# A scan followed by a mixture of adapters: one store more goes out in pieces, in a new order of work

## The chip, the cores and the metric

The kernel runs on one core of a Trainium2 chip. The metric is the device time of one execution in microseconds (us). The time before is the median of three runs, 202.56 us (202.31 to 202.83). An engine here is TensorE (PE, with its weight loads PEld), VectorE (DVE), ScalarE (ACT), GpSimd (POOL) or SyncE (SP). Sixteen DMA engines move the data; SP issues the transfers.

## The reference

```python
def _attn_ref(a, b):                      # a, b: (8, 6400, 128) float32
    h = np.zeros((B, D), dtype=np.float32)
    for t in range(S):
        h = a[:, t] * h + b[:, t]
        out[:, t] = h
    return out

def _moe_ref(x, w_gate, A, B):            # x: (51200, 128), 8 experts of rank 16
    logits = x @ w_gate
    topk = np.argpartition(-logits, K, axis=1)[:, :K]        # K = 2
    sel = np.take_along_axis(logits, topk, axis=1)
    w = np.exp(sel - sel.max(-1, keepdims=True))
    w /= w.sum(-1, keepdims=True) + 1e-09
    for e in range(E):
        for k in range(K):
            mask = topk[:, k] == e
            delta[mask] += w[mask, k, None] * (x[mask] @ A[e] @ B[e])
    return x + delta
```

A linear recurrence along 6400 steps for eight sequences gives 51200 rows of 128 values. Each row then goes through the two adapters that its gate picks, and their sum is added to it. The inputs a and b are 26.2 MB each, the output is 26.2 MB.

## The kernel before

The 51200 rows are cut into 100 chunks of 512 rows. A chunk goes through these steps. Names in parentheses are those of the kernel's operations, with the chunk's number behind them.

- SP loads a and b (la, lb, line 709), mostly for two chunks at a time, 512 KB each, into rings of six buffers.
- PE transposes them by products with a unit matrix (A, B, P, line 730), so that the 128 features lie on partitions and time along the free axis.
- ACT copies the transposed a out of PSUM (ae, line 748), and DVE runs the recurrence with its scan instruction (sc, line 786) from a_st and PSUM into xT. A scan needs the last column of the one before.
- PE multiplies xT by the eight A matrices and the gate (Z, line 806), ACT copies the products out (ze, line 812) in units of four or six blocks of 128 rows.
- A group of up to four units is gated: the two largest logits of a row are found and turned into weights in some eight small steps (g on DVE, q on POOL, w1 on ACT, lines 843 to 882).
- POOL or DVE multiplies the products by the weights (mu or md, lines 915 and 919), PE transposes that (T, line 928), ACT or DVE copies it to zwT (te, lines 934 and 937), PE adds xT and the adapters' outputs in PSUM (D, lines 942 and 943), ACT or DVE copies the sum into the ring outt (oe or od, lines 957 and 954).
- SP stores two chunks at a time, 512 KB, the last four chunks one by one (st, line 988). The store of chunks 80 and 81 is called store 80 below.

The order of the work on each of the five queues is worked out when the kernel is built. Every operation has a rank: the start of its period of six chunks, plus a number from `TEMPLATE` by its kind and its place in the period, plus a number of its own from `NUDGE`. `Program.schedule` walks through the operations with an estimated duration for each and, on each queue, takes the operation of the lowest rank among those still to be issued, with a window of zero. So the ranks alone decide the order on a queue, and the operations wait for each other by semaphores. Lists such as `TE_ACT`, `OE_DVE` and `GATE_DVE` say which engine does a copy or a step of the gating.

A store reads 128 partitions of outt; from each, two pieces of 2 KB, one for each chunk. `SPLIT` cuts a store by partitions into several DMAs, issued one after another by SP and counted on one semaphore. Before the change it holds store 68 alone, cut into 124 and 4 partitions:

```python
cuts = SPLIT.get(c, [128])
lows = [sum(cuts[:i]) for i in range(len(cuts))]

def send():
    all = [eng["sp"].dma_start(dst[p : p + n], view[p : p + n]) for p, n in zip(lows, cuts)]
    return all if len(all) > 1 else all[0]
```

At the end of SP's queue stand the waits for all stores. SP's last entries before the change are: lb98, then the stores 64, 68 (two DMAs), 66, 70, 72, 74, 76, 78, 80, 82, 84, 86, 90, 88, 92, 94, 98, 97, 99 and 96.

Of the kernel before, what the change touches and what calls it, by code (L numbers as in the profile page):

```python
# [218 lines left out]
EARLY = -400  # L219
LEAD = [1, 2]  # L220
TAPER = [2, 1, 1, 1, 1]
GATE_DVE = ['2_0', '2_14', '2_18', '3_1', '3_11', '3_13', '3_15', '3_16', '3_2', '3_8', '5_14', '5_17', '6_0', '6_18', '6_3', '7_1', '7_17', '7_18', '7_20', '7_21']
TAIL_UNITS = [4, 4, 4, 4]
HEAD_UNITS = [4, 4, 4]
FLAT = []
# [3 lines left out]
OE_DVE = [11, 15, 72, 81, 92, 94, 97]  # L229
# [13 lines left out]
SPLIT = {68: [124, 4]}  # L243
# [863 lines left out]
```

## Time and profile before

| what | value |
|---|---|
| median of three runs | 202.56 us (202.31 to 202.83) |
| the profiled execution: its time | 202.71 us |
| the profiled execution: its span, first to last instruction | 200.9 us |
| granted TensorE clock | 0.992 |
| busy PE / PEld / DVE / ACT / POOL | 179.4 / 156.7 / 175.8 / 175.7 / 136.6 us |
| DMA: moved, mean rate over the span | 79.26 MB, 395 GB/s |
| read from HBM, written to it | 52.56 MB, 26.21 MB |

The span is what the rows of the profile add up to. The time of the run also holds what lies before the first and behind the last instruction, 1.8 us here. A row of an engine gives line, engine, operation, the tile written and the tiles read, their shapes, the count, the busy time, the mean duration and the idle time of the engine before it with what ended it. A row of SP's queue marks the issue of a DMA, not its transfer; an issue's duration includes the time for which SP was held up in it. "To landing" is from the start of an issue until the last of the sixteen DMA engines has reported.

### The profile page before, as it was taken

The numbers are of one execution on the slowest core, as the hardware profiler recorded it, in microseconds if no ns is written. First come the engines' busy times: TensorE is split into PE (matmuls) and PEld (weight loads), VectorE is DVE, ScalarE is ACT, GpSimd is POOL, SyncE is SP. The second block draws the span as 40 slices with busy tenths as digits, with TensorE's granted clock in tenths as the row PEclk, the third lists the DMA queues.
The fourth block names the chain that finished last, engine by engine and source line by source line (L and its number), as shares of the span: only waits on it lengthen the run. The fifth ranks groups of instructions, "written<-read, shape, count | busy, mean of one in ns | idle before, by whom it ended". The sixth has DMA issues, their size and how long they took to land.

```text
span 200.9 us, 7616 instructions
## 1 busy us (share of the span) xinstructions
PE 179.4 (89%) x3192; PEld 156.7 (78%) x3192; DVE 175.8 (88%) x283; ACT 175.7 (87%) x327; POOL 136.6 (68%) x176
## 2 busy tenths in 40 slices
PE   6988888999899989996998999889999998998970
PEld 6876767888678878886887888778887887887850
DVE  1599899999999988998797999898899999999970
ACT  2479898999879989998897999899989998999870
POOL 1331549598999988697787797867956657867320
PEclk9999999999999999999999999999999999999996
DMA  6999999999999999999999999999999999999985
GB/s 211 399 410 405 407 409 402 409 409 404 420 400 402 393 415 404 408 413 411 408 412 409 410 409 416 413 409 410 412 410 409 417 411 408 402 385 385 373 339 203
DMA packets 29065, 79.26 MB, mean 395 GB/s; under 512 B 2664, under 2 KB 2920, under 8 KB 29032
## 3 DMA queue, kind: packets, MB, share of 16 engines
q1 hardware_dynamic: 28456, 78.39, 98.9%
q8 instruction: 25, 0.41, 0.8%
q10 hardware_dynamic: 576, 0.40, 0.6%
q14 instruction: 8, 0.07, 0.1%
HBM read 52.56 MB, written 26.21 MB: 392 GB/s over the span
## 4 chain that ended last, share of the span: by engine, by line
DMA 33%; PE 28%; ACT 8%; DVE 8%; issue 1%; SPq 1%; ACTq 0%
DMA a_tm<-in_a_dram 26%; DMA b_tm<-in_b_dram 7%; PE pO L942 5%; PE pZ L806 4%; PE pB L730 4%; PE pA L730 4%; DVE xT L786 4%; PE pO L928 4%; PE pO L943 4%; ACT zl L812 3%; ACT a_st L748 2%; ACT outt L957 2%; ACT zwT L934 1%; DVE zwT L937 1%; SPq L709 1%
## 5 line engine op out<-in xcount | busy, mean ns | idle before, releaser
L786 DVE TENSOR_TENSOR_SCAN xT<-a_st,xT,pB 128x512 f16<-128x512 f32 x96 | 120.5, 1255 | 6.5 <-PE pA L730 2.9
L915 POOL TENSOR_TENSOR zw<-zl,g 128x512 f16<-128x512 f32 x88 | 92.7, 1066 | 26.5 <-DVE g L882 19.3
L730 PE MATMUL pB<-ident_f,b_tm 64*128 64x64 f32 (+1 forms) x784 | 69.6, 230 | 6.1 <-DMA a_tm<-in_a_dram 5.6
L730 PE MATMUL pA<-ident_f,a_tm 64*128 64x64 f32 (+1 forms) x784 | 69.7, 230 | 0.6 <-DMA b_tm<-in_b_dram 0.3
L748 ACT COPY a_st<-pA 128x512 f32<-128x512 f32 x100 | 62.9, 634 | 4.9 <-PE pA L730 3.6
L730 PEld LDWEIGHTS pB<-ident_f,b_tm 64*128 64x128 f32 (+1 forms) x784 | 56.7, 139 | 11.1 <-DMA a_tm<-in_a_dram 7.3
L812 ACT COPY zl<-pZ 128x816 f32<-128x816 f32 (+1 forms) x69 | 59.6, 863 | 2.4 <-PE pZ L806 2.3
L730 PEld LDWEIGHTS pA<-ident_f,a_tm 64*128 64x128 f32 (+1 forms) x784 | 56.8, 139 | 6.1 <-DMA b_tm<-in_b_dram 0.7
L957 ACT COPY outt<-pO 128x512 f32<-128x512 f32 x87 | 55.0, 641 | 2.5 <-PE pO L943 2.2
L942 PE MATMUL pO<-ident_h,xT 128*128 128x128 f16 x368 | 51.4, 222 | 1.3 <-ACT zwT L934 1.1
L943 PE MATMUL pO<-cst_h,zwT 128*128 128x128 f16 x368 | 50.3, 219 | 0.0
L942 PEld LDWEIGHTS pO<-ident_h,xT 128*128 128x128 f16 x368 | 40.3, 113 | 4.4 <-ACT zwT L934 1.6
L806 PE MATMUL pZ<-cst_h,xT 128*128 128x136 f16 x400 | 36.0, 225 | 4.0 <-DVE xT L786 2.0
L943 PEld LDWEIGHTS pO<-cst_h,zwT 128*128 128x128 f16 x368 | 36.8, 100 | 0.0
L928 PE MATMUL pO<-ident_h,zw 128*128 128x128 f16 x368 | 35.2, 220 | 1.4 <-DVE outt L954 0.5
L806 PEld LDWEIGHTS pZ<-cst_h,xT 128*128 128x128 f16 x400 | 26.2, 115 | 8.6 <-DVE xT L786 4.2
L928 PEld LDWEIGHTS pO<-ident_h,zw 128*128 128x128 f16 x368 | 22.7, 97 | 4.9 <-issue 1.3
L937 DVE COPY zwT<-pO 128x512 f16<-128x512 f16 x57 | 23.0, 409 | 4.0 <-PE pO L928 3.6
L934 ACT COPY zwT<-pO 128x512 f16<-128x512 f16 x35 | 21.8, 627 | 4.4 <-PE pO L928 4.0
L852 POOL TENSOR_TENSOR L<-k,m 128x192 f32<-128x192 f32 (+2 forms) x16 | 8.3, 519 | 6.5 <-DVE m L850 6.5
L874 POOL TENSOR_TENSOR k<-k,L 128x192 f32<-128x192 f32 (+1 forms) x17 | 9.4, 554 | 4.5 <-DVE L L870 3.2
L848 POOL TENSOR_TENSOR L<-L,k 128x192 f32<-128x192 f32 (+1 forms) x15 | 8.6, 576 | 5.4 <-DVE L L845 4.7
(58 smaller groups left out, 113.3 us busy)
## 6 DMA issues: line engine op xcount, KB each, us to landing
a_tm<-in_a_dram SPq DMA_DIRECT2D x48, 512.0 KB, 13.1
b_tm<-in_b_dram SPq DMA_DIRECT2D x48, 512.0 KB, 13.2
out_dram<-outt SPq DMA_DIRECT2D x47, 512.0 KB, 13.1
a_tm<-in_a_dram SPq DMA_DIRECT2D x4, 256.0 KB, 4.2
out_dram<-outt SPq DMA_DIRECT2D x4, 256.0 KB, 4.0
b_tm<-in_b_dram SPq DMA_DIRECT2D x3, 256.0 KB, 5.7
out_dram<-outt SPq DMA_DIRECT2D x1, 496.0 KB
b_tm<-in_b_dram ACTq DMA_DIRECT2D x1, 256.0 KB, 3.4
```

The lines of the kernel that those rows point to most:

```text
L730: last = eng["pe"].transpose(*args)
L748: lambda: eng["act"].copy(a_st[c % NA][:, :], pA[:, c % 2, :]), fr(c, "ae"))
L786: last = eng["dve"].tensor_tensor_scan(out=x[:, s0:s1], data0=a_st[c % NA][:, s0:s1], data1=pB[:, c % 2, s0:s1], initial=init, op0=ALU.mul ...
L806: last = eng["pe"].matmul(pZ[:, k // (n // 2), o : o + W], xblock(b0 + k), Awg_h)
L812: return eng["act"].copy(zl[:, zb : zb + n, :].rearrange("p (h k) w -> p h (k w)", h=2), pZ[:, :, 0 : n // 2 * W])
L915: lambda: eng["pool"].tensor_tensor(out=wv, in0=zv, in1=gv, op=ALU.mult), ba(gi, c, "mu"))
L928: last = eng["pe"].transpose(ptile[:, k * 128 : k * 128 + 128], zz[:, k, :], ident_h[:, :])
L934: lambda: eng["act"].copy(zt, ptile[:, 0 : n * 128]), ba(gi, c, "ta"))
L937: lambda: eng["dve"].tensor_copy(zt, ptile[:, 0 : n * 128]), ba(gi, c, "te"))
L942: eng["pe"].matmul(dst, xblock(b0 + k), ident_h[:, :], start=True, stop=False)
L943: last = eng["pe"].matmul(dst, zt[:, k * 128 : k * 128 + 128], B_h, start=False, stop=True)
L957: lambda: eng["act"].copy(ov, bv), ba(gi, c, "oe"))
```

## The change

Store 80 goes out as five DMAs, of 112, 4, 4, 4 and 4 partitions, one behind the other on SP. The numbers in `TEMPLATE` and `NUDGE` are others for nearly every operation of the chunks 0 to 14 and 81 to 99; in between most `NUDGE` numbers are kept. Three lists change by a few entries:

```diff
-GATE_DVE = ['2_0', '2_14', '2_18', '3_1', '3_11', '3_13', '3_15', '3_16', '3_2', '3_8', '5_14', '5_17', '6_0', '6_18', '6_3', '7_1', '7_17', '7_18', '7_20', '7_21']
+GATE_DVE = ['2_0', '2_14', '2_17', '2_18', '3_1', '3_11', '3_13', '3_15', '3_16', '3_8', '5_14', '6_1', '6_18', '6_3', '7_17', '7_18', '7_20', '7_21']
-TE_ACT = [0, 1, 2, 6, 7, 11, 12, 19, 22, 24, 25, 30, 31, 36, 37, 42, 43, 48, 49, 54, 55, 59, 60, 61, 67, 68, 69, 73, 75, 78, 80, 82, 83, 87, 92, 93, 95, 96, 97, 98]
+TE_ACT = [0, 1, 2, 3, 6, 7, 11, 12, 19, 22, 24, 25, 30, 31, 36, 37, 42, 43, 48, 49, 54, 55, 59, 60, 61, 67, 68, 69, 73, 75, 78, 80, 82, 83, 87, 90, 92, 94, 95, 96, 97, 98]
-OE_DVE = [11, 15, 72, 81, 92, 94, 97]
+OE_DVE = [11, 15, 72, 81, 92, 93, 97]
-SPLIT = {68: [124, 4]}
+SPLIT = {68: [124, 4], 80: [112, 4, 4, 4, 4]}
 TEMPLATE = {
-    "la": [0.617, 1.382, -0.181],
-    "lb": [0.289, -1.881, 0.376],
+    "la": [1.746, 3.64, 1.589],
+    "lb": [1.687, 4.099, 0.505],
...
```

In the order that results, SP's queue is the same from the loads of chunk 66 on but for single places: the stores 66 and 70 stand ahead of 68, and store 94 ahead of 92. Its beginning is another: the loads of chunks 1 to 4 change places, store 0 goes out one pair of loads earlier, the stores 6 to 32 are spread otherwise among the loads of the chunks 34 to 64. On PE, DVE, ACT and POOL the order in the middle changes by single places; from chunk 88 on, the copy zwT of chunk 90 moves from DVE to ACT, the copies te and oe of chunks 93 and 94 exchange engines, of gating group 17 step 2 moves from POOL to DVE and step 5 from DVE to POOL.

More of the change, by code (lines that the diff above doesn't have):

```diff
@@ L242 @@
 STORE_TAIL = [1, 1, 1, 1]
-SPLIT = {68: [124, 4]}
+SPLIT = {68: [124, 4], 80: [112, 4, 4, 4, 4]}
 TOP8 = 4
 TEMPLATE = {
-    "la": [0.617, 1.382, -0.181],
-    "lb": [0.289, -1.881, 0.376],
-    "A": [0.0, 0.0, 0.0, 0.0, -22.609, 0.0],
-    "B": [0.016, -0.127, 0.808, 0.22, 0.59, 0.13],
-    "ae": [0.478, 0.108, 0.156, -0.214, 0.098, 0.802],
-    "sc": [-0.352, 0.601, 0.068, 1.247, 29.666, -1.078],
-    "Z": [0.074, 0.124, 0.07, -0.415],
-    "ze": [0.146, 0.091, -0.438, 0.663],
-    "g1": [0.736],
-    "g2": [-2.194],
-    "g3": [-0.858],
-    "g4": [-0.178],
-    "g5": [18.025],
-    "g6": [22.851],
-    "w1": [-0.215],
+    "la": [1.746, 3.64, 1.589],
+    "lb": [1.687, 4.099, 0.505],
+    "A": [0.0, 0.0, 0.0, 0.0, -31.987, 0.0],
+    "B": [0.376, -0.259, 0.365, 0.223, 0.306, 0.283],
+    "ae": [0.288, 0.221, -0.565, -0.575, -0.748, 1.3],
+    "sc": [-1.218, -1.749, -0.677, 0.613, 73.34, -1.523],
+    "Z": [0.196, 0.307, -0.011, -0.479],
+    "ze": [0.568, -0.504, -0.295, 1.091],
+    "g1": [7.23],
+    "g2": [-13.685],
+    "g3": [-2.163],
+    "g4": [-1.781],
+    "g5": [37.108],
+    "g6": [2.612],
+    "w1": [-1.333],
     "w2": [0.0],
@@ L264 @@
     "p3": [0.0],
-    "mu": [1.432, -0.247, 0.712, 0.979, 0.638, 1.684],
-    "T": [-0.04, 0.011, 0.309, 0.056, 0.263, 0.069],
-    "te": [-0.194, -0.349, -1.1, 4.512, 0.878, -1.627],
-    "D": [0.293, 0.3, -0.403, 0.26, 0.471, 0.206],
-    "oe": [-0.17, -1.066, 0.732, 0.378, -0.33, -0.315],
-    "st": [2.655, 0.241, 1.338],
-    "ta": [0.113, -0.235, -1.676, 1.106, 0.524, -0.261],
-    "md": [60.131, 24.961, 1.624, -2.633, 1.124, -17.851],
+    "mu": [2.792, 1.422, 1.022, 0.819, -2.419, 23.251],
+    "T": [-0.04, 0.099, 0.385, 0.077, -0.176, 0.11],
+    "te": [-1.747, -1.628, -1.308, 25.611, -20.775, -2.473],
+    "D": [0.087, -0.303, -0.762, 0.351, 0.059, 0.409],
+    "oe": [-0.455, -0.794, 0.928, 0.458, -0.076, -0.107],
+    "st": [13.665, 13.152, 11.84],
+    "ta": [2.542, -0.856, 2.005, 1.573, 0.74, 0.176],
+    "md": [104.08, 22.016, 10.978, -13.03, 11.367, -27.633],
     "wu": [0.0],
     "fi": [0.0, 0.0, 0.0, 0.0, 0.0, 0.0],
-    "ch": [53.69],
-    "cm": [11.639],
-    "cc": [8.728],
+    "ch": [122.022],
+    "cm": [101.955],
+    "cc": [20.929],
     "mb": [0.0],
-    "q2": [-0.491],
-    "q3": [-4.197],
-    "q5": [-3.568],
-    "q6": [0.447],
-    "q7": [0.367],
+    "q2": [0.509],
+    "q3": [-4.622],
+    "q5": [-4.987],
+    "q6": [-0.544],
+    "q7": [-7.111],
     "q8": [0.0],
-    "g7": [19.938],
-    "g8": [-0.285],
+    "g7": [33.274],
+    "g8": [-0.524],
 }
```

344 rows, old and new, of the table NUDGE are left out of this document.

## The prediction

> **What bounds the kernel now.** I read the page first, its strip of forty slices and its list of queues, then the windows of the tail, then SP's issues there, then the chain of waits.
>
> ```profile
> DMA  6999999999999999999999999999999999999985
> GB/s 211 399 410 405 407 409 402 409 409 404 420 400 402 393 415 404 408 413 411 408 412 409 410 409 416 413 409 410 412 410 409 417 411 408 402 385 385 373 339 203
> ...
> q1 hardware_dynamic: 28456, 78.39, 98.9%
> q8 instruction: 25, 0.41, 0.8%
> ...
> q14 instruction: 8, 0.07, 0.1%
> ```
>
> Five engines are busy for 68 to 89%, but the DMA engines are full from the second slice on: 78.39 MB move at about 410 GB/s, which is 191 us of a span of 200.9. Only the last five slices fall off. The row q8 matters below: 25 packets of instructions take 0.8% of sixteen engines' time, 0.008 x 16 x 200.9 / 25 = 1.03 us each, and each sits on one DMA engine.
>
> ```profile
> 160.00:170.00 10.00, 9.25 (x169) 7.84 (x167) 9.59 (x15) 9.03 (x18) 6.20 (x9) 1.00 1.04 413
> 170.00:175.00 5.00, 4.67 (x93) 4.09 (x91) 5.00 (x9) 5.00 (x10) 4.18 (x6) 1.00 1.01 401
> 175.00:180.00 5.00, 5.00 (x93) 4.52 (x90) 4.93 (x9) 4.96 (x11) 3.45 (x6) 1.00 1.03 385
> 180.00:185.00 5.00, 4.36 (x66) 3.68 (x65) 5.00 (x21) 4.92 (x11) 3.89 (x5) 1.00 1.04 395
> 185.00:190.00 5.00, 4.89 (x80) 4.29 (x78) 4.46 (x20) 4.43 (x11) 2.53 (x9) 1.00 0.95 365
> 190.00:195.00 5.00, 3.91 (x62) 3.27 (x60) 4.47 (x10) 3.46 (x8) 1.17 (x2) 1.00 0.89 340
> 195.00:198.00 3.00, 0.60 (x11) 0.42 (x8) 0.06 (x1) 1.07 (x2) 0.00 (x0) 0.95 0.81 313
> 198.00:201.00 3.00, 0.00 (x0) 0.00 (x0) 0.00 (x0) 0.00 (x0) 0.00 (x0) 0.50 0.36 139
> ```
>
> The columns are window, length, busy time of PE, PEld, DVE, ACT and POOL, clock, the mean share of the sixteen DMA engines, GB/s. From 185 us the mean share falls under one although stores are still outstanding: some DMA engines are out of work while others are not. That is an imbalance between the sixteen, and the changed split acts on nothing else.
>
> To see it, the sixteen semaphore updates of a DMA (one for each engine that has finished) are set out in order. This is counted from the trace's semaphore updates, in us; the first column is the issue's start:
>
> ```
> 164.60 store of 64       171.89 171.96 172.16 172.55 172.77 173.41 173.61 175.00 175.32 176.75 176.90 176.91 176.94 177.03 177.32 178.34
> 165.76 store of 68, 124  176.87 177.68 178.78 179.47   (four only)
> 166.23 store of 68, 4    177.08 177.88 178.96 179.66   (four only)
> 169.92 store of 66       173.13 173.39 173.79 176.24 176.69 178.00 178.16 178.17 178.18 178.31 178.31 178.57 179.11 179.75 180.19 180.92
> 170.55 store of 70       174.36 ... 180.39 181.12 181.47 182.20
> 192.20 store of 94       195.76 ... 196.59 196.89 197.62 197.85
> 197.10 store of 96       199.61 199.62 199.62 199.63 199.64 199.65 199.65 199.66 199.67 199.69 199.70 199.72 199.74 199.76 200.18 200.43
> ```
>
> Three things stand there. Before the split the sixteen engines are 6.4 us apart. Both pieces of store 68 run on four engines only, the same four (0.18 to 0.21 us between the two pieces on each), and those four were ahead before and are 178.3 to 180.92 after, so that the laggard at 180.92 is now one of them. At the end fourteen engines finish within 0.15 us (199.61 to 199.76), just behind the last issue, and two are late: 200.18 and 200.43. Followed from row to row, a store costs most engines 1.24 to 1.28 us, and one engine outside the four, which I call X, 1.38 to 1.41 (178.34, 179.75, 181.12). X overtakes by store 94 and is the 200.43; the slowest of the four is the 200.18. The span ends 0.47 us later, the run at 202.71, 1.81 above the span; the median of the three runs is 202.56, 0.15 below the profiled one.
>
> **The change part by part.** *The split of store 80.* It goes out as one piece of 112 partitions and four of 4.
>
> ```profile
> out_dram<-outt SPq DMA_DIRECT2D x47, 512.0 KB, 13.1
> ...
> out_dram<-outt SPq DMA_DIRECT2D x1, 496.0 KB
> ...
> out_dram<-outt SPq DMA_DIRECT2D x1, 16.0 KB
> ```
>
> A whole store gives each engine 8 partitions of 4 KB in 1.28 us, 0.16 us each. The trace has no piece of 112. Its bounds are the two rows: spread over sixteen as 128 is (7 partitions an engine), or over four as 124 is (28 an engine). I take sixteen, since 112 divides by 16 as 128 does and 124 does not. Every engine then saves 0.16 us (X 1.40 / 8 = 0.18). The four pieces of 4 all fall on the four: by data 4 x 0.16 = 0.64 us, by the measured 0.18 to 0.21 of the existing piece 0.72 to 0.84. I take 0.19 each, 0.76, the measured middle. The four get 0.76 - 0.16 = +0.60 us (0.48 to 0.68), the other twelve -0.16, X -0.18.
>
> In the Trainium skill, "DMA: Bandwidth & Descriptors", section "Why a DMA increments its semaphore by 16 and not by 1", a DMA takes the largest number up to 16 that divides the slowest dimension of both sides, on the lowest-numbered engines. The fours of updates above agree with it for 124 and 4; no row here shows it for 112, where it gives sixteen. [...]
>
> *SP's issues.* Four more of them.
>
> ```profile
> L988 SPq DMA_DIRECT2D out_dram<-outt x1: 3641/3641/3641, 166.2 to 166.2; - x1
> ...
> L988 SPq DMA_DIRECT2D out_dram<-outt x2: 1248/1329/1410, 178.9 to 180.2; - x2
> ...
> DMA to landing us min/median/max: 9.8/9.8/9.8
> ...
> L988 SPq DMA_DIRECT2D out_dram<-outt x2: 982/1050/1118, 195.9 to 197.1; - x2
> ...
> DMA to landing us min/median/max: 3.3/3.6/3.8
> ```
>
> The existing piece of 4 took 3.64 us to issue, behind 31 partitions for each of four queues; behind 7 partitions the first of the new ones should cost no more than an ordinary issue, and each of the others 0.35 to 0.5: some 2 us for SP at 180. Store 82, queued behind, takes 9.8 us from issue to landing against 3.3 for the last one, so some 6 us of queued work cover it on the slow engines. The fourteen quick ones do run dry, but end with the last issue at 197.10 anyway. If the cover were gone it would cost those 2 us. I count zero.
>
> *The new order on the five queues.* From the loads of chunk 66 on SP's order stands as before but for single places; ahead of that loads and stores change places by a few (store 0 goes out a pair of loads earlier, store 16 much earlier).
>
> ```profile
> 93.66 12.68 DMA a_tm<-in_a_dram
> ...
> 133.18 13.83 DMA a_tm<-in_a_dram
> ...
> 152.79 13.74 DMA b_tm<-in_b_dram
> ...
> 166.52 0.04 issue
> 166.57 0.27 PE pA L730
> ```
>
> The chain of waits comes back to a load again and again, for the last time at 166.57: compute has caught up with the loads there, and a load sits 12 to 14 us in the queue. A wait early in SP's queue has that queue as its cover; lost cover costs the length of the wait less that queue. So the early reordering counts zero, with no gain to be had either, as the DMA engines have no gap there.
>
> After 166.57 the chain is compute to the end, and there the moves are few: the copy of zwT of chunk 90 goes from DVE to ACT, 93 and 94 change engines for both copies, one step of a gating moves to POOL and another to DVE.
>
> ```profile
> L937 DVE COPY zwT<-pO 128x512 f16<-128x512 f16 x57 | 23.0, 409 | 4.0 <-PE pO L928 3.6
> L934 ACT COPY zwT<-pO 128x512 f16<-128x512 f16 x35 | 21.8, 627 | 4.4 <-PE pO L928 4.0
> ...
> 185.57 0.42 DVE L937 COPY zwT<-pO 128x512 f16<-128x512 f16 x1 [0.40 <-PE pO L928]
> 185.91 0.41 DVE L937 COPY zwT<-pA 128x512 f16<-128x512 f16 x1
> 186.46 0.42 DVE L937 COPY zwT<-pO 128x512 f16<-128x512 f16 x1
> ...
> 186.24 0.59 ACT L957 COPY outt<-pA 128x512 f32<-128x512 f32 x1 [0.36 <-PE pA L943]
> ```
>
> DVE loses 0.41 us, but stood waiting 0.40 us for PE just before; ACT gains 0.63, and has 0.36 of idle time there. The last issue moves by -0.4 to +0.3 us; I take zero. This counts only for the fourteen quick engines, which end at 199.76, 0.67 before the last.
>
> **The sum.** X: 200.43 - 0.18 = 200.25. The slowest of the four: 200.18 + 0.60 = 200.78 (200.66 to 200.86). The quick ones: 199.76 (199.4 to 200.1). The last landing goes from 200.43 to 200.78, +0.35, the profiled run to 203.06, the median to 202.9 (by the bounds 202.8 to 203.0).
>
> **The rivals.** A difference of 0.3%, 0.6 us, is about what a measurement of this kernel can tell from no change.
>
> *X stays last.* If the four come to store 80 with less lag, the end is X's 200.25: 202.56 - 0.18 = 202.4. For it: 173.41 and 173.61 in the row of store 64 become 178.78 and 179.47, 5.4 and 5.9 us for what cost the other two 4.9, so the laggard carries up to 1 us that need not come back. Against: the same kernel repeats within 0.5 us.
>
> *Faster.* The 25 packets of instructions hold one DMA engine each for 1.03 us, and queue q14's smaller ones less; which engine they hit makes the spread of 6.4 us. With a new order of instructions one can leave X, and another the slowest of the four: 200.25 - 1.03 = 199.2 and 200.78 - 0.95 = 199.8. The quick engines would decide together with the latter, 199.8: -0.63 us; with up to 0.4 from an earlier last issue, 201.8 in the middle. For it: fourteen engines are ready by 199.76. Against: it needs both at once.
>
> *Slower.* The same packet falls on the slowest of the four behind the split, while the late engines have no idle time left: 200.78 + 1.03 = 201.8, +1.4 us, 203.9. It decides from 0.6 us of extra wait on those four engines. For it: three such packets start after 176 us here (176.2, 181.9 and 191.0 by the trace's packet records), and the change makes four engines late instead of two. Against: two of the four have 0.4 us and more in hand.
>
> *It doesn't do what it says.* If the piece of 112 runs on four engines as 124 does, each gets 28 + 4 partitions instead of 8, 24 x 0.16 = 3.8 us: 204.0 against 200.43, +3.6 us, 206.1.
>
> **How the numbers follow.** Forecast 0.36, X stays last 0.08: together 0.44 for no difference over 0.3%. Faster 0.20. Slower 0.30 by a late packet and 0.06 by four engines, together 0.36. The likeliest is 202.9, its own range 202.4 to 203.2. With the rivals at 201.8 and 203.9 and the 0.1 to 0.2 us that single runs differ, 201.7 to 204.1; outside are the 0.06 at 206.1 and the ends of the rivals.
>
> **What would show it.** The page lists one more row of 448 KB and five rows or counts of 16 KB. The updates of the 112 piece come sixteen at a time (right) or four (the last rival). In the store of 96, two or more engines land late by 0.5 to 1.2 us behind the other twelve, and they are of the four that land the pieces of 4; if a single one is late, X has stayed last. The last issue of SP stands within 0.4 us of 197.1. Wrong would be a last issue later than 197.8, a gap in the DMA strip before slice 35, or all sixteen engines landing together.

## The result, and the profile after

The changed kernel takes 204.89 us (204.58 to 205.54, four runs) against 202.69 for the kernel before (202.31 to 202.83, four runs): a ratio of 1.0113, 95% interval 1.0091 to 1.0136. It is 2.2 us slower, and above the upper end of the forecast's range. Its profiled run took 205.54 us, with a span of 203.5 and a granted clock of 0.985.

The strips of the page's forty slices, after:

```profile
DMA  5999999999999999999999999999999999995995
GB/s 214 345 417 404 411 407 404 409 407 407 411 413 408 411 414 407 407 405 415 406 411 402 412 413 410 417 409 409 411 414 409 409 421 405 378 384 196 345 385 218
```

Where the kernel before ran down smoothly (385 385 373 339 203), there is now a hole of one slice, 196 GB/s, and after it the rate comes back to 385. The windows of the tail place it:

```profile
175.00:180.00 5.00, 5.00 (x93) 4.51 (x91) 4.97 (x9) 4.96 (x11) 4.14 (x6) 1.00 1.00 380
180.00:185.00 5.00, 4.40 (x66) 3.70 (x64) 5.00 (x21) 4.92 (x12) 3.62 (x5) 1.00 0.99 363
185.00:190.00 5.00, 4.57 (x80) 4.28 (x78) 4.13 (x19) 4.78 (x12) 2.53 (x9) 1.00 0.52 179
190.00:195.00 5.00, 3.94 (x62) 3.29 (x60) 4.47 (x11) 3.54 (x9) 1.26 (x3) 1.00 1.01 375
195.00:198.00 3.00, 0.68 (x13) 0.50 (x10) 0.13 (x1) 1.07 (x2) 0.00 (x0) 0.90 1.03 388
198.00:204.00 6.00, 0.00 (x0) 0.00 (x0) 0.00 (x0) 0.00 (x0) 0.00 (x0) 0.50 0.56 214
```

From 185 to 190 us the sixteen DMA engines are busy for 0.52 of the time, where they were for 0.95: 5 x 0.43 = 2.15 us lost. That is near the 2.2 us of the median, but the two need not be equal, since the rate behind the hole is higher than it was before (375 and 388 GB/s for 340 and 313). In the hole itself the last column says 179 GB/s for 365. The busy times of PE, DVE and ACT there differ from those before by 0.3 to 0.4 us, but the computation does not end late. The last copy into outt shows it, first before and then after:

```profile
195.67 0.59 ACT L957 COPY outt<-pA 128x512 f32<-128x512 f32 x1
...
195.75 0.59 ACT L957 COPY outt<-pA 128x512 f32<-128x512 f32 x1
```

It ends at 196.34, 0.08 later than before. What was late is SP's queue. Its rows at line 988 after, first the five DMAs of store 80, then everything from store 82 on (minimum, median and maximum of an issue in ns, start of the first and the last):

```profile
L988 SPq DMA_DIRECT2D out_dram<-outt x5: 947/1442/1840, 180.0 to 186.1; - x5
...
L988 SPq DMA_DIRECT2D out_dram<-outt x11: 468/1193/2118, 187.1 to 199.3; - x11
```

The five took 1.44, 1.84, 1.63, 1.01 and 0.95 us and held SP from 180.00 to 187.04. Before, store 80 was one issue of 1.25 us, and store 82 went out at 180.15. Now it goes out at 187.09, 6.94 us later. Behind it SP does not catch up: eleven issues follow one another with a median of 1.19 us and never wait for a copy, so that the last goes out at 199.33 instead of 197.10. The sixteen updates of the last store, in us:

```
before 199.61 ... 199.76 (fourteen) 200.18 200.43
after  201.76 ... 201.89 (eleven)   202.02 202.35 202.45 202.57 203.07
```

The quick engines end 2.2 us later, as the last issue does (2.23). The chain of waits does not show this: it ends in ACT's queue, at 195.72 after and 195.64 before, and follows no store.

The list of DMA issues after shows the split as written:

```profile
out_dram<-outt SPq DMA_DIRECT2D x14, 512.0 KB, 9.3
...
out_dram<-outt SPq DMA_DIRECT2D x1, 448.0 KB
out_dram<-outt SPq DMA_DIRECT2D x5, 16.0 KB
```

### The profile page after: what moved, and what is told of

It reads as the page before. It is cut to its first block, busy times and chain, and to the rows that moved or that the text cites. A ratio compares the mean times of both kernels' runs of the same rounds, so it can differ in the third digit from the quotient of the medians.

```text
span 203.5 us, 7626 instructions
## 1 busy us (share of the span) xinstructions
PE 179.8 (88%) x3192; PEld 156.3 (77%) x3192; DVE 174.5 (86%) x279; ACT 176.8 (87%) x329; POOL 138.4 (68%) x178
## 4 chain that ended last, share of the span: by engine, by line
DMA 26%; ACT 26%; PE 22%; DVE 11%; issue 4%; SPq 4%; POOL 3%; ACTq 0%; DVEq 0%
DMA a_tm<-in_a_dram 20%; ACT outt L957 8%; DVE xT L786 7%; ACT a_st L748 7%; ACT zl L812 6%; DMA b_tm<-in_b_dram 6%; ACT zwT L934 4%; PE pA L730 4%; PE pO L942 4%; PE pZ L806 4%; SPq L709 3%; PE pO L928 3%; PE pB L730 3%; PE pO L943 3%; POOL zw L915 3%
## 5 line engine op out<-in xcount | busy, mean ns | idle before, releaser
L957 ACT COPY outt<-pO 128x512 f32<-128x512 f32 x88 | 56.5, 650 | 2.9 <-PE pO L943 2.8
L937 DVE COPY zwT<-pO 128x512 f16<-128x512 f16 x55 | 22.3, 409 | 3.4 <-PE pO L928 3.2
L934 ACT COPY zwT<-pO 128x512 f16<-128x512 f16 x37 | 22.9, 627 | 2.0 <-PE pO L928 1.6
L874 POOL TENSOR_TENSOR k<-k,L 128x192 f32<-128x192 f32 (+2 forms) x18 | 9.7, 539 | 4.7 <-DVE L L852 3.6
L848 POOL TENSOR_TENSOR L<-L,k 128x192 f32<-128x192 f32 (+2 forms) x16 | 9.0, 564 | 4.3 <-DVE L L845 3.5
L786 DVE TENSOR_TENSOR_SCAN xT<-a_st,pB 128x512 f16<-128x512 f32 (+1 forms) x8 | 7.5, 937 | 4.6 <-PE pB L730 4.6
```

The lines of the kernel that those rows point to most:

```text
L786: last = eng["dve"].tensor_tensor_scan(out=x[:, s0:s1], data0=a_st[c % NA][:, s0:s1], data1=pB[:, c % 2, s0:s1], initial=init, op0=ALU.mul ...
L934: lambda: eng["act"].copy(zt, ptile[:, 0 : n * 128]), ba(gi, c, "ta"))
L937: lambda: eng["dve"].tensor_copy(zt, ptile[:, 0 : n * 128]), ba(gi, c, "te"))
L957: lambda: eng["act"].copy(ov, bv), ba(gi, c, "oe"))
```

## The experiments

Two kernels stand for "before's ranks" and "after's ranks"; the only line that is edited is `SPLIT`, and the ranks are all other lines of the diff. Every ratio is to the kernel before on the same chip, with its 95% interval; that kernel's own median was 202.50 to 202.64. The ratio is not the quotient of the two medians; it differs from it by up to 0.0024. The time for which SP was held is the time from the start of a store's first issue to the end of its last. The theory to be tested was that SP's slow issues make the loss; its rivals were the imbalance of the DMA engines and the new ranks.

**The ranks alone, and the split alone.** With after's ranks:

```diff
-SPLIT = {68: [124, 4], 80: [112, 4, 4, 4, 4]}
+SPLIT = {68: [124, 4]}
```

> The changed kernel's ranks with store 80 whole again. Theory H (hold): the five DMAs of store 80 hold SP for 7.0 us in their issue (180.00 to 187.04) where a whole store takes 1.3; nine stores behind them go out late, the DMA engines' mean share falls to 0.52 in 185 to 190, and the end moves by 5 x (0.95 - 0.52) = 2.2 us. Then this kernel has no hold, store 82 goes out near 181.5, and it runs in 202.5 to 202.9 us. Theory F (forecast: the four engines get 0.6 us more): 204.3. Theory R (the new ranks are slower): 204.9 as the changed kernel.

With before's ranks:

```diff
-SPLIT = {68: [124, 4]}
+SPLIT = {68: [124, 4], 80: [112, 4, 4, 4, 4]}
```

> The kernel before with the split of store 80 alone added. H: the five DMAs hold SP for some 7 us here too, 204.4 to 205.3 us. F: 203.0 to 203.3. R: 202.7, as before.

The ranks alone: 202.89 us, ratio 1.0011 (0.9997 to 1.0026), no difference that can be told. The split alone: 204.84 us, 1.0125 (1.0075 to 1.0175), the whole loss. SP's five issues and the windows of the split alone:

```profile
L988 SPq DMA_DIRECT2D out_dram<-outt x5: 1116/1200/2031, 179.0 to 184.7; - x5
```

```profile
180.00:185.00 5.00, 4.36 (x66) 3.70 (x65) 5.00 (x21) 4.86 (x11) 3.88 (x6) 1.00 0.95 351
185.00:190.00 5.00, 4.90 (x81) 4.33 (x79) 4.46 (x20) 4.49 (x10) 2.51 (x9) 1.00 0.63 216
190.00:195.00 5.00, 3.92 (x61) 3.28 (x59) 4.39 (x10) 3.33 (x8) 1.06 (x1) 1.00 1.02 379
```

SP was held from 179.01 to 185.91, and the hole is there again (0.63). What the new ranks do can be left aside.

**Fewer pieces, and pieces without imbalance.** Both with after's ranks.

```diff
-SPLIT = {68: [124, 4], 80: [112, 4, 4, 4, 4]}
+SPLIT = {68: [124, 4], 80: [112, 16]}
```

> The changed kernel's ranks, store 80 as two DMAs of 112 and 16 partitions. 16 partitions should report from sixteen engines, one partition each, so that no engine gets more than another. H, with a hold for each DMA issued: one hold in place of four, 1.3 to 1.9 us more than whole: 202.8 to 203.5. F: no imbalance, as whole, 202.6 if the ranks cost nothing. R: 204.9.

```diff
-SPLIT = {68: [124, 4], 80: [112, 4, 4, 4, 4]}
+SPLIT = {68: [124, 4], 80: [32, 32, 32, 32]}
```

> The changed kernel's ranks, store 80 as four DMAs of 32 partitions, each over sixteen engines with two partitions for each: no imbalance, as many bytes for each engine as a whole store. H1 (each DMA waits for a place in a full queue that an earlier DMA frees, whatever its size): SP held about 5 us, 203.8 to 204.6. H2 (SP waits for room for the bytes or descriptors of the pieces on the engine that is furthest behind): hardly more than whole, 202.6 to 203.0. F: 202.6, no imbalance. R: 204.9.

112 and 16: 204.12 us, 1.0073 (1.0054 to 1.0092). SP was held for 2.9 us (178.71 to 181.63), the share of 185 to 190 is 0.94, and the last issue is at 196.95, so the hole is gone. But two engines end at 201.82 and 201.91, the other fourteen by 199.86, and none of the three theories had this time; what keeps those two was not settled.

Four quarters: 203.24 us, 1.0047 (1.0025 to 1.007). All sixteen engines share each piece, so there is no imbalance, and still:

```profile
L988 SPq DMA_DIRECT2D out_dram<-outt x4: 1391/1517/1728, 178.6 to 183.4; - x4
```

```profile
180.00:185.00 5.00, 4.40 (x65) 3.72 (x64) 5.00 (x21) 4.92 (x11) 3.61 (x5) 1.00 0.94 344
185.00:190.00 5.00, 4.57 (x81) 4.28 (x79) 4.13 (x19) 4.78 (x12) 2.53 (x9) 1.00 0.83 300
```

A quarter of a store holds SP as long as a whole one, 6.3 us for the four: the hold is that of H1, and longer, and the time lies between H1 and H2. The time grows by 0.35 us only, since the four went out from 178.65 on instead of 180.00 and store 82 at 184.97 instead of 187.09. From there SP still catches up: it waits for copies again at 191.75 and 194.33, and its last issue is at 197.20. So a long hold can be cheap when SP catches up before the last copy.

**The same split later, where less is queued.** Before's ranks.

```diff
-SPLIT = {68: [124, 4]}
+SPLIT = {68: [124, 4], 86: [112, 4, 4, 4, 4]}
```

> The kernel before, with store 86 as 112, 4, 4, 4 and 4 partitions, and store 80 whole. Store 86 goes out at 185.9 after SP has stood 2.4 us with nothing ready, when the queue is no longer full. H1 (a DMA waits for a place that an earlier DMA frees on the slowest engine; no wait while there are places): the five issues take 0.4, 1.1, 0.4, 0.4 and 0.4 us, SP is done near 188.5, store 90 goes out almost as before, no hole in the DMA share; 202.6 to 203.3 us, the rest by the four engines' 0.6 us. H3 (each small DMA has a fixed price of 1 to 1.8 us on SP): SP is held until 191 to 193, 204.3 to 205.5.

204.84 us, 1.0102 (1.0068 to 1.0137). The five issues:

```profile
L988 SPq DMA_DIRECT2D out_dram<-outt x5: 335/1061/2042, 185.2 to 190.0; - x5
```

The 112 went in 0.33 us, after SP had waited; the four small ones still took 1.16, 2.04, 1.06 and 0.68, 5.4 us in all, and the DMA share of 190 to 195 falls to 0.72, where it was 0.89. That a small DMA is cheap where the queue is not full fell.

**What the split of store 68 is worth, and where the late engine sits.** Before's ranks, three kernels.

```diff
-SPLIT = {68: [124, 4]}
+SPLIT = {}
```

> The kernel before with no store cut at all. The issue of store 68 then holds SP for about 1.3 us and not 4.1. The engine that ends last before (X, 200.43) has to write one whole store more, 1.3 to 1.4 us, and the four engines 3.8 us less: 203.8 to 204.1 us, one engine landing late. If SP's hold at 68 cost more than the balance gained: under 202.3.

```diff
-SPLIT = {68: [124, 4]}
+SPLIT = {68: [120, 8]}
```

> The kernel before with store 68 as 120 and 8 partitions in place of 124 and 4. 120 is 15 x 8, so that fifteen engines get as much as from a whole store and one gets nothing; the 8 fall on eight engines, one partition each. If the spared engine is X: X 200.43 + 1.35 (store 68 no longer on four engines) - 1.35, the four engines 3.5 us earlier; other laggards as with whole stores: 202.4 to 202.8 us. If it is another engine: X one store later, 203.8 to 204.1. One more place in SP's queue either way, as before.

```diff
-SPLIT = {68: [124, 4]}
+SPLIT = {68: [120, 8], 74: [120, 8]}
```

> The kernel before with the stores 68 and 74 both as 120 and 8. If the spared engine is X, it gains two stores against whole ones and one against the kernel before: X near 199.1, and the last landing is the quick engines' 199.7: 201.9 to 202.2 us, unless the hold of SP for one DMA more (1.3 to 1.6 us) comes through. If another engine is spared: 203.8 to 204.3.

Unsplit: 203.29 us, 1.0021 (0.9997 to 1.0044), between the two times expected. One engine alone is late, 201.38, the next ends at 199.87 and fourteen by 198.69. With one split in 120 and 8: 203.83, 1.0042 (1.0022 to 1.0063); with two: 203.63, 1.0034 (1.0014 to 1.0053), a little under what was expected; the late engine is still at 201.62 and 201.51. By the count of the semaphore's updates the 120 ran on fifteen engines and the 8 on eight, so the late engine was not the one left out; the last two updates of this store, 179.79 and 180.00, are its eight rows and one row of the 8 behind them.

The unsplit kernel showed something else. Its last four issues, and the place where store 68's piece of 4 had taken 3.64 us before:

```profile
L988 SPq DMA_DIRECT2D out_dram<-outt x4: 332/342/344, 194.3 to 196.3; - x4
...
DMA to landing us min/median/max: 5.0/5.1/5.2
...
L988 SPq DMA_DIRECT2D out_dram<-outt x2: 514/2216/3917, 165.7 to 166.3; - x2
```

The same four stores cost the kernel before up to 1.12 us each:

```profile
L988 SPq DMA_DIRECT2D out_dram<-outt x4: 350/898/1118, 194.4 to 197.1; - x4
...
DMA to landing us min/median/max: 3.3/4.0/4.1
```

So a split thirty microseconds earlier decides what a later issue costs. It is not that more work lies ahead of these stores on the slowest engine: they land 3.3 to 4.1 us after their issue there, and 5.0 to 5.2 us in the unsplit kernel, whose issues are quick. And the hold of some 3.6 us at 166 was no price of the split: a whole store pays 3.92 there.

**How long that lasts, and which pieces do it.** Before's ranks, four kernels.

```diff
-SPLIT = {68: [124, 4]}
+SPLIT = {0: [124, 4]}
```

> Kernel of before without the split of store 68, but with store 0, the first, split in 124 and 4 partitions. After the unsplit kernel SP passed its last four stores in .34 us each; with the split of 68 the last three cost .81 to 1.12 us each. Theory A (a DMA on fewer than sixteen engines leaves every later issue slow, for good): the last four issues cost .8 to 1.1 us again, and the time is 203.3 to 204. Theory B (slow issues come from what is queued at the time, so a piece 100 us earlier is forgotten): the last four issues cost .3 to .5 us, and the time is that of the unsplit kernel, 203.0 to 203.5.

```diff
-SPLIT = {68: [124, 4]}
+SPLIT = {68: [64, 64]}
```

> Store 68 as two pieces of 64 partitions, both on sixteen engines, so one DMA more and no imbalance. Theory A (only DMAs on fewer than sixteen engines slow SP): the last four issues cost .34 us, the late engine is as late as in the unsplit kernel, 203.0 to 203.6. Theory C (each further DMA costs SP 1 to 1.8 us whatever its size, and that is felt only where the engines' queues run dry behind it): the pieces of 68 cost 1.1 to 1.8 us each, there is queued work behind them, and the time is the same 203.0 to 203.6; the two differ in the issues of the last four stores alone.

```diff
-SPLIT = {68: [124, 4]}
+SPLIT = {80: [32, 32, 32, 32]}
```

> Store 80 as four pieces of 32 partitions, and store 68 whole: no DMA of the tail on fewer than sixteen engines. Theory A: the four pieces together hold SP for about 2.5 us, store 82 goes out by 182, and the time is the unsplit kernel's, 203.0 to 203.6. Theory C: the four hold SP for 5.5 to 6.5 us as they did with the split of 68 (178.65 to 184.93), store 82 goes out at about 185, the DMA share of 185 to 190 falls below .9, and the time is 203.6 to 204.6.

```diff
-SPLIT = {68: [124, 4]}
+SPLIT = {72: [119, 9], 80: [119, 9]}
```

> Stores 72 and 80 as 119 and 9 partitions, on seven and on nine engines if the number of engines is the largest divisor of the rows up to sixteen; the split of 68 is gone. The late engine of the unsplit kernel was not spared by pieces of eight engines, and was by those of four, so it is one of the fifth to the eighth. If it is the eighth, both splits spare it by about 1.2 us each (a store takes it 1.40 us, 9 rows some .4), and the time is 201.9 to 202.5 if SP's issues stay hidden. If it is one of the fifth to the seventh it gets more than its share of both: 204 to 206. If SP's slow issues decide (Theory C: two more DMAs, 1 to 2 us each, and room for them at 170 but not at 181): 203 to 204.

The last four issues with store 0 split, with halves of 68, and with quarters of 80:

```profile
L988 SPq DMA_DIRECT2D out_dram<-outt x4: 332/341/345, 194.0 to 195.9; - x4
```

```profile
L988 SPq DMA_DIRECT2D out_dram<-outt x4: 332/344/382, 194.8 to 196.7; - x4
```

```profile
L988 SPq DMA_DIRECT2D out_dram<-outt x4: 332/350/396, 194.2 to 196.1; - x4
```

All three are quick. So a split 170 us earlier is forgotten ("for good" fell), and pieces on all sixteen engines do not slow the issues far behind them. Store 0 itself shows where the price stands. In that kernel the two pieces at 26.5 took

```profile
L988 SPq DMA_DIRECT2D out_dram<-outt x2: 360/3170/5980, 26.5 to 26.9; - x2
```

0.36 for the 124 and 5.98 for the 4 behind it, where the unsplit kernel passed the whole store in 0.98 and the load behind it in 0.47.

The quarters of store 80 are to be set beside the quarters above, where store 68 was split as well and the ranks were those of after:

```profile
L988 SPq DMA_DIRECT2D out_dram<-outt x4: 570/746/1252, 177.5 to 180.1; - x4
```

1.25, 0.57, 0.64 and 0.86, 3.4 us for the four instead of 6.3, and store 82 goes out at 180.95: theory A's figure of 2.5 was short by 0.9, C's 5.5 to 6.5 is out. The times: store 0 split 202.20, 0.997 (0.9945 to 0.9995), less than either theory had; halves 203.29, 1.003 (1.0007 to 1.0054); quarters 203.48, 1.0046 (1.0027 to 1.0064).

119 and 9 twice: 207.31 us, 1.0235 (1.019 to 1.028), above all that was expected. The updates count seven engines for the 119 and nine for the 9, so that seven got 2 x 10 rows more than their share. The two engines that got the 9 alone were the first to report (176.65 and 176.75), so the late one is none of them. If a DMA on fewer engines always takes the first ones of a fixed order, it is one of the fifth to the seventh in that order; the trace does not number the engines. The pieces of 80 took 1.57 and 1.53 us, the last issues as long as in the change, and the hole is back:

```profile
185.00:190.00 5.00, 4.89 (x81) 4.33 (x79) 4.86 (x19) 4.63 (x11) 2.04 (x6) 1.00 0.65 211
...
L988 SPq DMA_DIRECT2D out_dram<-outt x4: 1157/1200/1257, 196.0 to 199.8; - x4
```

**The change without the split of store 68**, and the early split again. Before's ranks.

```diff
-SPLIT = {68: [124, 4]}
+SPLIT = {80: [112, 4, 4, 4, 4]}
```

> Store 80 in 112 and four times 4 partitions, as in the change, but store 68 whole. Theory D (the slow issues of the change come from the split of store 68 before it): the five DMAs hold SP for 3.5 us or less, as four quarters did without that split (178.76 to 181.8 after the first), store 82 goes out before 183, and the time is near the unsplit kernel's 203.3, at most 203.8. Theory E (each DMA on fewer than sixteen engines costs SP 1 to 2 us by itself): they hold it 5.5 to 7.5 us, store 82 goes out after 184.5, the DMA share of 185 to 190 falls below .75, and the time is 204.3 to 205.5.

203.36 us, 1.0035 (1.0019 to 1.005). The five DMAs:

```profile
L988 SPq DMA_DIRECT2D out_dram<-outt x5: 430/784/939, 177.5 to 180.6; - x5
```

```profile
180.00:185.00 5.00, 4.36 (x66) 3.68 (x65) 5.00 (x21) 4.92 (x11) 3.88 (x5) 1.00 1.01 383
185.00:190.00 5.00, 4.89 (x80) 4.29 (x78) 4.46 (x20) 4.43 (x11) 2.53 (x9) 1.00 0.93 345
```

0.94, 0.78, 0.79, 0.43 and 0.53: 3.65 us from 177.52 to 181.17, store 82 out at 181.21, no hole. This is theory D but for 0.15 us of hold; E's 5.5 to 7.5 us, its share under 0.75 and its time fell. The same five DMAs cost 0.1 us beside the unsplit kernel (203.36 against 203.29, beside kernels before of 202.59 and 202.50), and 2.3 where store 68 was split before them (204.84 against the 202.57 of the kernel before): the two splits do not add.

```diff
-SPLIT = {68: [124, 4]}
+SPLIT = {0: [124, 4]}
```

> The kernel with store 0 alone in 124 and 4 partitions once more, in more rounds. If the one late engine of the unsplit kernel (201.38, the others 199.9 and less) is set forward for good by the row of work that this split spares it: 201.9 to 202.4, ratio .996 to .999. If the first result was chance: 202.7 to 203.4, ratio 1.000 to 1.004.

```diff
-SPLIT = {68: [124, 4]}
+SPLIT = {0: [124, 4], 20: [124, 4]}
```

> Stores 0 and 20 both in 124 and 4 partitions, store 68 whole. If what counts is how much work the late engine is spared by then: about 1.2 us less on it and 3.6 us more on four others, which then end last at 201 to 202: 203 to 205. If an early imbalance is evened out by the waits of the loads behind it: as with store 0 alone, 201.9 to 202.6.

Store 0 alone, on another chip: 202.57 us, 0.9993 (0.9979 to 1.0007). The first result's gain did not come again; here this kernel cannot be told from the one before, and no other kernel of the study is faster. It is below the unsplit 203.29, which neither expectation had. Stores 0 and 20 both: 207.37 us, 1.0225 (1.0201 to 1.0249), worse than either expectation. Here the loss is not in the tail:

```profile
195.00:198.00 3.00, 2.35 (x41) 2.11 (x38) 3.00 (x9) 2.35 (x7) 1.42 (x3) 1.00 0.75 279
198.00:203.00 5.00, 2.41 (x36) 1.84 (x33) 1.78 (x4) 2.43 (x5) 0.00 (x0) 1.00 1.02 385
```

PE works until after 198, some 5 us later than in every other kernel, while the sixteen updates of the last store stand within 1.6 us. The page and SP's queue show where the time went. The piece of 4 of store 20, issued at 71.37, held SP for 7.55 us, and right behind it the strip has a hole, as the change has one:

```profile
L988 SPq DMA_DIRECT2D out_dram<-outt x1: 7550/7550/7550, 71.4 to 71.4; - x1
...
DMA  6999999999999995999999999999999999999885
GB/s 214 396 408 408 411 405 401 405 411 409 412 407 408 412 405 234 324 350 372 409 416 405 414 409 414 408 415 411 409 410 415 408 413 408 409 398 388 312 324 219
```

With store 0 alone split, store 20 went out whole in 0.44 us at the same place. The four slices of 234, 324, 350 and 372 GB/s, 5.15 us each, are short of some 410 by 360 together, which is 0.88 of a slice, 4.5 us: nearly the whole 4.8 us by which this kernel is slower than the one with store 0 alone. Why this piece was held so long is as open as for the others.

The kernels that bear on SP's issues, side by side:

| `SPLIT`, ranks | us | ratio | SP held by the split store | last four issues, us | last landing |
|---|---|---|---|---|---|
| 68, before | 202.50 to 202.69 | 1 | - | 0.35 to 1.12 | 200.43 |
| 68, after | 202.89 | 1.0011 | - | 0.35 to 1.09 | 199.99 |
| 68 and 80 in 112, 4, 4, 4, 4, after (the change) | 204.89 | 1.0113 | 7.0 | 0.93 to 1.26 | 203.07 |
| the same, before | 204.84 | 1.0125 | 6.9 | 0.89 to 1.29 | 202.28 |
| 68 and 80 in quarters, after | 203.24 | 1.0047 | 6.3 | 0.42 to 1.17 | 200.90 |
| 68 and 86 in 112, 4, 4, 4, 4, before | 204.84 | 1.0102 | 5.4 | 0.62 to 1.28 | 202.30 |
| none, before | 203.29 | 1.0021 | - | 0.33 to 0.34 | 201.38 |
| 80 in quarters, before | 203.48 | 1.0046 | 3.4 | 0.33 to 0.40 | 201.37 |
| 80 in 112, 4, 4, 4, 4, before | 203.36 | 1.0035 | 3.65 | 0.35 to 0.81 | 200.78 |

## Why the prediction was wrong

**The step that failed is SP's issues.** It said "some 2 us for SP at 180", "some 6 us of queued work cover it", "I count zero". Three things in it were off.

The price. Five DMAs held SP for 7.0 us, where one had held it for 1.25: 5.8 us more and not 2. The existing piece of 4 was read as the worst case, 3.64 us behind 31 partitions for each of four queues, from which the new ones were to be cheaper. The unsplit kernel passes a whole store at that place in 3.92 us, so that row measured what any DMA pays there and said nothing on pieces. And "0.35 to 0.5" for each of the rest is what the last four issues cost in a kernel whose DMAs all use sixteen engines (0.33 to 0.40); at 180 us even there a quarter cost 0.57 to 1.25. Behind store 68's split most issues that follow one another cost 0.9 to 1.8 us whatever their size, as the two kernels with quarters show (6.3 and 3.4 us), and the five DMAs of the change with and without that split (6.9 and 3.65). The hint stood in the quoted row of the last two issues, "982/1050/1118": 256 KB, little queued, and a microsecond each. It was used as the start of the last issue and not asked why it was so long.

The cover. Six microseconds were taken from the time between the issue of store 82 and its last landing, 9.8. That is the queue of the slowest engine, and the prediction itself said so ("on the slow engines"), but it let the quick ones go for the next reason. On the quickest three the same store had landed 3.8 us after its issue (183.91 against 180.15), and a store that finds an engine idle needs 2.6 us there from issue to landing (store 86: 188.55 against 185.91): 1.1 us of cover. On the middle engines, which landed at 187.13, it is 4.3 us. The hold moved store 82 by 6.94.

The end of the quick engines. "The fourteen quick ones do run dry, but end with the last issue at 197.10 anyway" takes the last issue as set by the copies. With eleven issues at 1.19 us behind 187.09 SP itself became the bound from 180 us on: 187.09 + 11 x 1.19 = 200.2, and the last issue ended at 200.26. The prediction had named this case ("if the cover were gone it would cost those 2 us") and its sign, a last issue later than 197.8, but gave it no chance among the rivals. That 2 us was also the loss is luck: the working reached it with a price three times too small.

**The balance of the engines** was right in its mechanism. The 112 came in sixteen updates. In the Trainium skill, "DMA: Bandwidth & Descriptors", section "Why a DMA increments its semaphore by 16 and not by 1", the largest divisor up to sixteen gives that; the counts of updates here agree for 112 (sixteen), 120 (fifteen), 119 (seven) and 9 (nine). The pieces of 4 took 0.18 to 0.20 us each on an engine (190.04, 190.24, 190.43, 190.61), as taken. In the last store five engines, as many as the four and X, are 0.1 to 1.2 us behind eleven quick ones. This was the term that the sum of +0.35 rested on, and it is the smaller one: the last engine is 1.18 us behind the quick ones (203.07 against 201.89), where it was 0.67, so that some 0.5 us come on top of quick engines that end 2.2 us late.

**The new ranks** were counted as zero, and are: 202.89 against 202.57 with an interval that holds 1. The last issue of that kernel is at 196.73, -0.37 from 197.10, within the stated -0.4 to +0.3.

**The rivals.** That the 112 runs on four engines did not happen. The slower rival had the right side with another cause: a packet of instructions on the slowest of the four. As many such packets run after as before (25), one of them holds one engine, while eleven engines ended 2.2 us later here, and the split alone, without the new order of instructions, gives the same loss. That these packets make the spread of 6.4 us between the engines no run shows: 25 of 1.03 us are 1.6 us for each engine in the mean. A gap in the strip came in the thirty-seventh slice, not before the thirty-fifth.

**What stays open.** Shown is that the split of store 68 into 124 and 4 partitions makes the issues behind it slow up to the end of the queue, with the split and without it in the same place, and that a split of store 0 is forgotten by then. What lets it be forgotten is not shown: the DMA strip of that kernel has no gap in between, so the queue was not seen to run empty. The small pieces on four engines do it little by themselves (last four issues 0.35 to 0.81 in the change without the split of 68), one split over fifteen and eight hardly. Why SP is held by that was not shown. Room in the queues of the slowest engine would explain the normal 1.2 to 1.6 us of a whole store, but not a piece of 4 partitions that takes as long, nor the quick last issues of the unsplit kernel, whose slowest engine has more ahead of it. Still, SP may keep step with that engine: in the change six issues in a row end 0.15 to 0.19 us after the DMA four places ahead has landed on its last engine (191.76 to 198.08), while with the split alone the distance drifts. Open too are the two late engines of the kernel with 112 and 16, and why a split at store 0 makes the late engine of the unsplit kernel less late 170 us after it.

## What to carry to other kernels

When a store is cut, price its pieces on the queue that issues them, one by one and through to the last issue: there a piece of 16 KB may cost what 512 KB cost, and the queue that had slack becomes the bound. Read the cover from the engine that lands first, not from the last landing, and take off what a store needs on an idle engine. Two splits that are each harmless or useful can cost 2 us together, so a split is tried with the others in place and alone.

## What the hardware showed that was not expected

- In the tail, where 256 KB go out at a time, an issue costs 0.33 to 0.40 us when every DMA of the last 40 us used sixteen engines. With store 68 in 124 and 4 partitions the last four cost up to 1.09 to 1.29, with two stores in 119 and 9 they cost 1.16 to 1.26, and with one store in 120 and 8 they cost 0.34 to 0.56.
- One DMA engine takes 1.40 us for a store in the mean of nine (1.33 to 1.44, from 178.30 to 190.90 in the unsplit kernel), where most others take 1.24 to 1.28; in that kernel it ends 1.5 us behind the next. At the very end it is no slower than the others (0.61 to 0.65 us for 256 KB).
- A DMA on four engines early in the kernel costs nothing in the end when it is alone (202.20 and 202.57), and 4.8 us when a second follows while the loads still run (207.37): SP stood for 7.55 us in one piece of 16 KB.
